# Products with c of five double tiles made ahead in a fused convolution and spectral-mix kernel, and stored tiles put in other places

## Chip, cores, metric

One core of a Trainium2 chip. The metric is the device time of one execution in microseconds, as a median of several runs. The profiler's span, from the first to the last instruction of one execution, is about 1.8 us shorter.

In the views, PE is the TensorE engine with its matmuls, DVE is VectorE, ACT is ScalarE, and POOL is GpSimd, which here issues most of the DMAs. SBUF is the memory that DMAs and engines share, PSUM the one into which PE writes. "X <-Y" in brackets is an idle time and what ended it.

## The reference, cut to what matters

```python
# x: (8, 3264, 192); w: softmax over 7 taps for 8 groups of 24 channels
x = causal_conv(x, w)                          # _attn_ref
X = rfft(x, axis=1)[:, :64]                    # 64 modes
Y = X @ (w_r + 1j * w_i)  per mode             # the weights: 64 x 192 x 192, twice
y = irfft(Y, n=3264)
u = x + y
out = u + relu(u @ w_ch)
```

The kernel never forms u @ w_ch from u. It adds c = x @ w_ch and y @ w_ch in PSUM.

## The kernel before

Three stages follow each other: the convolution with the forward transform (to about 72 us), the mixing with the weights, which come in 16 groups (to about 107 us), and the output stage. The output stage runs over items. Most are double tiles: two tiles of 128 rows for two batches, 384 KB of output. One item is made of the half tiles ("h") and three are "zw" tiles for the inverse transform. Each item takes one of four PSUM tiles of two banks in turn. The names C, M0 and M1 below are the parts of PE's work for an item. The code is cut and simplified; the cuts are marked by "...".

```python
xall  = sb("xall", [NSLOT, 2, D], BF16, align_bytes=256)
arena = sb("arena", [NW * WGB], BF16, align_bytes=256)   # weights, later stored tiles
cc    = sb("cc", [NQ, CB, P], BF16)                      # x transposed, for C
band  = sb("band", [H, 2 * P], BF16)                     # taps of the convolution
NO = 6
outs = [arena[:, OB * i:OB * (i + 1)]... for i in range(NO)]   # six places of 3072 bytes
outs.append(band[...])                                         # and one for the halves
...
def c_part(n):      # C: 12 matmuls, c of a double tile
    ... matmul(zt[:, i, D*k:D*k+D], cc[r, q, 3*t+j, :], wc[r, j, :], start=(k == 0 and j == 0))
def m_part(n, which):   # M0 = y @ w_ch, M1 = y: 4 matmuls of 384 columns each
def relu(n):        # ScalarE, in place in PSUM, 128x768 f32
def finish(n):      # VectorE adds x into a stored tile in SBUF, then a DMA stores it
...
for n in range(N + 1):
    m_part(n, 0); relu(n)
    if duos[n + 2] == ("h",): nc.scalar.copy(out=<PSUM tile of n + 2>, in_=halves)
    c_part(n + 1)
    m_part(n - 1, 1); finish(n - 1)
```

Of the kernel before, what the change touches and what calls it, by code (L numbers as in the profile page):

```python
# [12 lines left out]
F32 = mybir.dt.float32  # L13
# [6 lines left out]
def kernel(  # L20
# [9 lines left out]
    nc = tc.nc  # L30
    B, S, D = x.shape
# [5 lines left out]
    P = 128  # L37
# [15 lines left out]
    def sb(name, shape, dtype, **kw):  # L53
        return pool.tile([P] + shape, dtype, tag=name, name=name, **kw)
# [4 lines left out]
    NW = 4  # L59
    WGB = 4 * 3 * D  # L60
    arena = sb("arena", [NW * WGB], BF16, align_bytes=256)

    CB = 3 * NT
    cc = sb("cc", [NQ, CB, P], BF16)
# [13 lines left out]
    band = sb("band", [H, 2 * P], BF16)  # L78
# [3 lines left out]
    wc = sb("wc", [3, D], BF16)  # L82
# [11 lines left out]
    def wbuf(g):  # L94
        return wts[g] if g < NW + NL else wts[(g - NW - NL) % NW]

    NO = 6
    OB = 2 * 2 * 2 * D
    outs = [arena[:, OB * i:OB * (i + 1)].bitcast(F32).rearrange("p (k d) -> p k d", k=2) for i in range(NO)]
    assert NO * OB <= NW * WGB  # L100

    outs.append(band[:, :, :].rearrange("p h c -> p (h c)")[:, 0:OB].bitcast(F32).rearrange("p (k d) -> p k d", k=2))
    pos = [0]

    def temp(n, dtype):
# [36 lines left out]
    def slot(q, t):  # L142
        return NT * q + t
# [210 lines left out]
    tbank = [0]  # L354
    ncopy = [0]

    def copy(out, in_):
        ncopy[0] += 1
        if ncopy[0] % 3 == 0:
            nc.scalar.copy(out=out, in_=in_)  # L360
        else:
            nc.vector.tensor_copy(out=out, in_=in_)  # L362

    ring = low[2:4]

    def next_bank():
        z = ring[tbank[0] % len(ring)]
        tbank[0] += 1
        return z[:, :].bitcast(BF16)
# [29 lines left out]
    def some(n, upto=NT * NQ):  # L399
        for _ in range(n):  # L400
            if tjobs and tjobs[0][0] < upto:
                _, f, *a = tjobs.pop(0)
                f(*a)
# [3 lines left out]
    for k, u in enumerate(units):  # L407
# [5 lines left out]
        if k:  # L413
            q, t0, n = units[k - 1]
# [19 lines left out]
    def mix(g):  # L434
        yp = low[(g // 2) % 2][:, D * (g % 2):D * (g % 2) + D]
        for j in range(3):
            for p4 in range(4):
                m = 4 * g + p4
                nc.tensor.matmul(yp[32 * p4:32 * p4 + 2 * B, :], xt[:, j, :, m],  # L439
                                 wbuf(g)[:, p4, j, :], start=(j == 0), stop=(j == 2),  # L440
                                 tile_position=(0, 32 * p4), skip_group_check=True)
        if g < NW:
            load_w(g + NW + NL)
        elif g >= NW + NL:
            load_w(g + NW)
            if g + NW == NG - 1:

                small(0)
                small(1)

    def mix_copy(d, gs=slice(0, 2)):
        nc.scalar.copy(out=ymix[d % 2][:, gs, :],
                       in_=low[d % 2][:, 0:2 * D].rearrange("p (g d) -> p g d", g=2)[:, gs, :])
# [25 lines left out]
    ROWS = (LO, UP)  # L479
# [4 lines left out]
    def c_halves():  # L484
        for k in range(2):
# [8 lines left out]
                                         tile_position=(r.start, h.start))  # L494
            copy(halves[:, 2 * k:2 * k + 2, :], z[:, 0:2 * D].rearrange("p (a d) -> p a d", a=2))

    def c_part(n, ks=(0, 1)):
        duo, zt = items[n]
        for k, (q, t) in enumerate(duo):
            for j in range(3) if k in ks else ():  # L500
                for i, r in enumerate(ROWS):
                    nc.tensor.matmul(zt[:, i, D * k:D * k + D], cc[r, q, 3 * t + j, :], wc[r, j, :],  # L502
                                     start=(k == 0 and j == 0), stop=False, skip_group_check=True)
# [28 lines left out]
    def zw_copy(dst, src, act):  # L532
        if act:
            nc.scalar.activation(out=dst, in_=src, func=ACT.Copy, scale=ascale[:, 0:1])
        else:
            nc.vector.tensor_scalar(out=dst, in0=src, scalar1=ascale[:, 0:1], scalar2=None, op0=ALU.mult)

    duos = [((q, t), (q, t + 1)) for q in range(2) for t in (0, 2)]
# [3 lines left out]
    for k, item in ((2, 1), (8, 2), (11, 3), (14, ("h",))):  # L542
        duos.insert(k, item)

    buffers = []
    for duo in duos:
        buffers.append(NO if duo == ("h",) else sum(b < NO for b in buffers if b is not None) % NO
                       if isinstance(duo, tuple) else None)

    def relu(n):  # L550
        duo, zt = items[n]
        w = D * len(duo) if duo[0] != "h" else 2 * D
        nc.scalar.activation(out=zt[:, :, 0:w], in_=zt[:, :, 0:w], func=ACT.Relu)  # L553

    def finish(n):
        duo, zt = items[n]
        o = outs[buffers[n]]
        if duo[0] == "h":
            nc.vector.tensor_tensor(out=o[:, :, :].rearrange("p k (a d) -> p k a d", a=2),
                                    in0=zt[:, :, 0:2 * D].rearrange("p k (a d) -> p k a d", a=2),  # L560
                                    in1=xall[:, NF:NF + NT * (NQ - 1) + 1:NT, 0, :].rearrange(
                                        "p (k a) d -> p k a d", k=2), op=ALU.add)
            for k in range(2):
                for h, r in enumerate(ROWS):
                    dst = bass.AP(tensor=out.tensor, offset=out.offset + ((4 * k + (h ^ k)) * S + P * NF) * D,
                                  ap=[[D, HALF], [2 * S * D, 2], [1, D]])
                    nc.sync.dma_start(out=dst, in_=o[r, k, :].rearrange("p (a d) -> p a d", a=2))
            return
        (q0, t0), (q1, t1) = duo[0], duo[-1]
        s = [slot(*u) for u in duo]  # L570
        ov = o[:, :, :].rearrange("p k (i d) -> p (k i) d", i=2)
        if len(duo) == 1:
            nc.vector.tensor_tensor(out=ov[:, 0:2, :], in0=zt[:, :, 0:D], in1=xall[:, s[0], :, :], op=ALU.add)
            dst = bass.AP(tensor=out.tensor, offset=out.offset + (2 * q0 * S + P * t0) * D,
                          ap=[[D, P], [S * D, 2], [1, D]])
            (nc.gpsimd if n < N - 1 else nc.sync).dma_start(out=dst, in_=ov[:, 0:2, :])
            return
        nc.vector.tensor_tensor(out=o[:, :, :].rearrange("p k (i d) -> p i k d", i=2),  # L578
                                in0=zt[:, :, 0:2 * D].rearrange("p i (k d) -> p i k d", k=2),
                                in1=xall[:, s[0]:s[1] + 1:s[1] - s[0], :, :].rearrange("p k i d -> p i k d"),  # L580
                                op=ALU.add)
        if t0 == t1:

            dst = bass.AP(tensor=out.tensor, offset=out.offset + (2 * q0 * S + P * t0) * D,
                          ap=[[D, P], [S * D, 4], [1, D]])
            nc.gpsimd.dma_start(out=dst, in_=ov)  # L586
        else:
            for i in range(2):
                dst = bass.AP(tensor=out.tensor, offset=out.offset + ((2 * q0 + i) * S + P * t0) * D,
                              ap=[[D, P], [P * D, 2], [1, D]])  # L590
                nc.sync.dma_start(out=dst, in_=ov[:, i:4:2, :])

    N = len(duos)
    items = [[duo, None] for duo in duos]
# [3 lines left out]
            if k % 4 in Z:  # L598
                item[1] = Z[k % 4]

    PLAN = (2, 2, 1, 2, 2, 2, 1, 2, 3, 3, 3, 3, 3, 3, 99)
    for g in range(NG - 1):
        mix(g)
        if g == NG - 2:
            mix_copy(g // 2, slice(0, 1))
        elif g % 2:
            mix_copy(g // 2)
        some(PLAN[g], NT * (NQ - 1) if g < NW + NL - 1 else NT * NQ)
        if g == NG - 2:
            c_halves()  # L610
        if g == NG - 2:
            mix_trans(g // 2, slice(0, 1))
        elif g % 2:
            mix_trans(g // 2)
# [20 lines left out]
    def is_duo(n):  # L635
        return 0 <= n < N and isinstance(duos[n], tuple)

    for n in range(N + 1):
        if is_duo(n):
            m_part(n, 0)  # L640
            relu(n)
        if n + 2 < N and duos[n + 2] == ("h",):
            nc.scalar.copy(out=items[n + 2][1][:, :, 0:2 * D].rearrange("p k (a d) -> p k a d", a=2),
                           in_=halves.rearrange("p (k a) d -> p k a d", k=2))
        if n + 1 < N and n > 0:
            if is_duo(n + 1):
                if duos[n + 1] != ("h",):
                    c_part(n + 1)
            else:
                q, zt = items[n + 1]  # L650
                for c in range(2):
                    zw_part(q, c, zt[:, c, :])
                for act, w in enumerate(QUARTERS):
                    zw_copy(zw[:, q, :, w, :], zt[:, :, 0:2 * D].rearrange("p c (b e) -> p c b e", b=4)[:, :, w, :],
                            act)
        if is_duo(n - 1):
            m_part(n - 1, 1)
            finish(n - 1)
# [30 lines left out]
```

## Time and profile before

| | before |
|---|---|
| median of 6 runs | 180.06 us (179.76 to 180.76) |
| span of the profiled run | 178.0 us |
| last group of weights starts on PE | 106.93 us |
| last store issued | 172.22 us |
| PE, DVE, ACT busy from 150 to 160 us | 10.00, 8.45, 6.88 of 10 us |

The prediction below shows the lines that lead to its reading. One view that it read: busy time by stretch. Its columns are the stretch and its length, then the busy time of PE, PE's weight loads, DVE, ACT and POOL (with instructions), the granted clock, the DMA share, and GB/s.

```profile
140.00:144.00 4.00, 4.00 (x76) 3.15 (x72) 3.44 (x4) 2.94 (x4) 2.82 (x4) 1.00 0.98 373
...
148.00:152.00 4.00, 4.00 (x76) 3.15 (x74) 3.44 (x4) 2.92 (x4) 2.83 (x4) 1.00 0.91 344
...
156.00:160.00 4.00, 4.00 (x77) 3.15 (x74) 3.44 (x4) 2.90 (x4) 2.82 (x4) 1.00 0.90 344
```

PE is full and sets the pace. The DMA engines are at 0.90 to 0.98, so the stores keep up with little to spare: at 373 GB/s for a share of 0.98, full use would be about 380 GB/s by this estimate.

### The profile page before, as it was taken

To read this page: it belongs to the slowest core of one execution; us is meant where nothing else is said; L and a number is where in the kernel's file an instruction comes from. 1 tells how busy PE (TensorE), PEld (TensorE's weight loads), DVE (VectorE), ACT (ScalarE), POOL (GpSimd) and SP (SyncE) were. 2 spreads that over 40 slices of the span, in tenths; PEclk is the share of its full clock that TensorE was granted. 3 is DMA by queue.
4 is the path that set the end of the run, shared out by engine and by line. 5 is a ranking of instruction groups with operands and counts; after the bars stand their busy time and mean duration, and the time that the engine had idled before them with its cause. 6 is when DMAs were issued, how large, how long until landed. Compare 5 with 4: busy or idle time off the path is not lost.

```text
span 178.0 us, 6299 instructions
## 1 busy us (share of the span) xinstructions
PE 146.5 (82%) x2736; PEld 105.9 (59%) x2736; DVE 114.1 (64%) x163; ACT 99.5 (56%) x136; POOL 100.4 (56%) x155
## 2 busy tenths in 40 slices
PE   0047569999999999689967679999999999999930
PEld 0033346667666666467756556965777777777720
DVE  1878555675765576255454453796688888888870
ACT  8176653735553734365546355767766667766620
POOL 7999997867855624354226100035364766665760
PEclk9999987999999999999999999999999999999997
DMA  4999999999999999999999980296699899998894
GB/s 44 168 177 188 189 190 190 192 193 190 191 191 190 205 206 208 205 206 208 205 207 206 206 130 0 90 324 258 251 300 351 317 368 356 354 349 348 336 356 186
DMA packets 44331, 40.17 MB, mean 226 GB/s; under 512 B 28800, under 2 KB 40656, under 8 KB 44304
## 3 DMA queue, kind: packets, MB, share of 16 engines
q0 software_dynamic: 41136, 37.59, 106.0%
q1 hardware_dynamic: 3168, 2.19, 3.9%
q8 instruction: 21, 0.34, 0.7%
q14 instruction: 6, 0.05, 0.1%
HBM read 39.40 MB, written 20.05 MB: 334 GB/s over the span
## 4 chain that ended last, share of the span: by engine, by line
DMA 33%; POOL 32%; PE 16%; issue 13%; ACT 1%; POOLq 1%; DVE 1%; DVEq 0%
DMA arena<-in_moe_w_i_dram 19%; POOL out_dram L586 17%; POOL xall L151 10%; DMA xall<-in_x_dram 8%; DMA cc<-in_moe_w_i_dram 6%; PE z L307 4%; PE low L333 3%; PE za L522 2%; PE za L502 2%; POOL xall L221 1%; POOL arena L428 1%; PE zb L522 1%; PE zb L502 1%; ACT xall L325 1%; PE low L387 1%
## 5 line engine op out<-in xcount | busy, mean ns | idle before, releaser
L586 POOL DMA_DIRECT2D out_dram<-arena x45 | 33.9, 754 | 39.2 <-DVE arena L578 38.4
L151 POOL DMA_DIRECT2D xall<-in_x_dram x48 | 38.5, 813 | 6.7 <-DMA xall<-in_x_dram 4.6
L307 PE MATMUL z<-xall,band 64*64 64x192 bf16 (+3 forms) x816 | 27.8, 264 | 16.1 <-ACT band L195 10.5
L327 DVE CAST xall<-z 128x768 bf16<-128x768 f32 (+1 forms) x24 | 24.5, 1021 | 15.1 <-PE z L307 13.3
L307 PEld LDWEIGHTS <-band 64*64 64x64 bf16 x816 | 18.4, 111 | 24.8 <-ACT band L195 10.9
L325 ACT CAST xall<-z 128x768 bf16<-128x768 f32 (+1 forms) x24 | 20.4, 851 | 22.3 <-PE z L307 21.1
L502 PEld LDWEIGHTS <-cc 64*128 64x128 bf16 x600 | 26.2, 94 | 7.0 <-issue 1.2
L578 DVE TENSOR_TENSOR arena<-za,xall 128x768 f32<-128x768 f32 x26 | 24.8, 956 | 5.6 <-ACT zb L553 1.9
L553 ACT ACTIVATE za<-za 128x768 f32<-128x768 f32 (+1 forms) x27 | 21.0, 782 | 8.3 <-PE za L522 8.3
L578 DVE TENSOR_TENSOR arena<-zb,xall 128x768 f32<-128x768 f32 x23 | 21.9, 956 | 4.6 <-ACT za L553 1.8
L553 ACT ACTIVATE zb<-zb 128x768 f32<-128x768 f32 (+1 forms) x25 | 19.6, 782 | 8.4 <-PE zb L522 8.2
L333 PE MATMUL low<-xall,ftab 128*128 128x384 bf16 x100 | 21.7, 344 | 0.0
L387 PEld LDWEIGHTS <-xall 128*128 128x128 bf16 x300 | 18.7, 105 | 3.2 <-issue 0.3
L362 DVE COPY cc<-r 128x1024 bf16<-128x1024 bf16 (+2 forms) x18 | 11.2, 658 | 12.8 <-PE r L387 3.9
L502 PE MATMUL za<-wc,cc 64*128 64x192 bf16 x318 | 17.8, 243 | 0.0
L522 PE MATMUL za<-mixa,fsin 64*128 64x384 bf16 (+1 forms) x120 | 17.6, 304 | 0.0
L522 PE MATMUL za<-mixa,ftab 64*128 64x384 bf16 (+1 forms) x120 | 17.6, 304 | 0.0
L428 POOL DMA_DIRECT2D arena<-in_moe_w_r_dram x12 | 7.4, 615 | 15.4 <-PE low L439 10.3
L522 PE MATMUL zb<-mixa,ftab 64*128 64x384 bf16 (+1 forms) x100 | 15.6, 313 | 0.4 <-ACT zb L553 0.4
L502 PE MATMUL zb<-wc,cc 64*128 64x192 bf16 x282 | 15.6, 243 | 0.1
L522 PE MATMUL zb<-mixa,fsin 64*128 64x384 bf16 (+1 forms) x100 | 15.6, 313 | 0.0
L522 PEld LDWEIGHTS <-ftab 64*128 64x128 bf16 x220 | 11.0, 94 | 4.6 <-issue 1.7
(111 smaller groups left out, 184.2 us busy)
## 6 DMA issues: line engine op xcount, KB each, us to landing
out_dram<-arena POOLq DMA_DIRECT2D x45, 384.0 KB, 4.3
xall<-in_x_dram POOLq DMA_DIRECT2D x24, 192.0 KB, 7.4
xall<-in_x_dram POOLq DMA_DIRECT2D x16, 240.0 KB, 7.1
arena<-in_moe_w_r_dram POOLq DMA_DIRECT2D x12, 288.0 KB, 9.6
arena<-in_moe_w_i_dram POOLq DMA_DIRECT2D x12, 288.0 KB, 10.5
out_dram<-arena SPq DMA_DIRECT2D x9, 192.0 KB, 2.1
xall<-in_x_dram POOLq DMA_DIRECT2D x8, 144.0 KB, 7.1
cc<-in_moe_w_r_dram POOLq DMA_DIRECT2D x4, 288.0 KB, 11.5
```

The costliest lines, as they stand in the source:

```text
L151: nc.gpsimd.dma_start(out=xall[:, s0:s0 + nf, i, :], in_=src)
L307: mm = nc.tensor.matmul(ov[c], band[r, h, c.start + shift + 64 * (r is UP and c is LO): c.start + shift + 64 * (r is UP and c is LO) + 64] ...
L325: nc.scalar.copy(out=dst, in_=srcv)
L327: nc.vector.tensor_copy(out=dst, in_=srcv)
L333: nc.tensor.matmul(xp, ftab[:, t, :], xall[:, slot(q, t), :, :], start=(t == 0), stop=False, skip_group_check=True)
L362: nc.vector.tensor_copy(out=out, in_=in_)
L387: nc.tensor.transpose(tp[:, P * k:P * k + P], src, ident[:])
L502: nc.tensor.matmul(zt[:, i, D * k:D * k + D], cc[r, q, 3 * t + j, :], wc[r, j, :], start=(k == 0 and j == 0), stop=False, skip_group_check ...
L522: nc.tensor.matmul(zt[:, i, D * k:D * (k + w)], tabs[c][r, t, :], zw[r, q:q + w, c, QUARTERS[which], :], start=False, stop=end and k + w = ...
L553: nc.scalar.activation(out=zt[:, :, 0:w], in_=zt[:, :, 0:w], func=ACT.Relu)
L578: nc.vector.tensor_tensor(out=o[:, :, :].rearrange("p k (i d) -> p i k d", i=2), in0=zt[:, :, 0:2 * D].rearrange("p i (k d) -> p i k d", k=2),
L586: nc.gpsimd.dma_start(out=dst, in_=ov)
```

## The change

The output stage is bound by PE, and PE has room while the weights load. So the change makes C of five double tiles (items 6, 9, 12, 17, 20) in the weights' stretch and keeps it in f32 in SBUF. ScalarE copies it into the PSUM tile when its item is due. The kept products need room in the arena, so the stored tiles get other places too: two in the part of cc that is used up first, and one in the convolution's band. The transposes in the weights' stretch move to earlier groups.

```diff
-    NO = 6
-    outs = [arena[:, OB * i:OB * (i + 1)]... for i in range(NO)]
-    outs.append(band[...])
+    slices = [place(arena[:, OB * i:OB * (i + 1)]) for i in range(6)]
+    in_band = place(band[:, :, :].rearrange("p h c -> p (h c)")[:, 0:OB])
+    in_cc = [place(cc[:, q, 0:12, :].rearrange("p k s -> p (k s)")) for q in range(2)]
...
+    def c_ahead(n):          # C of item n into two banks, then two copies to AHEAD[n]
...
+    AHEAD = {6: in_band, 9: slices[0], 12: slices[1], 17: slices[2], 20: slices[3]}
+    FREED = {9: (6,), 13: (9, 12, 17), 14: (20,)}        # after which group of weights
+    free = [in_cc[0], slices[4], slices[5], in_cc[1]]
+    for n, duo in enumerate(duos):
+        if n + 1 in AHEAD:
+            free.insert(0, AHEAD[n + 1])
+        buffers.append(None)
+        if isinstance(duo, tuple):
+            buffers[n] = free.pop(0)
+            free.append(buffers[n])
...
-    PLAN = (2, 2, 1, 2, 2, 2, 1, 2, 3, 3, 3, 3, 3, 3, 99)
+    PLAN = (2, 2, 3, 2, 3, 2, 2, 2, 3, 3, 3, 3, 99, 99, 99)
...
+        if n + 2 in AHEAD:
+            nc.scalar.copy(out=items[n + 2][1][:, :, 0:2 * D], in_=AHEAD[n + 2])
-                if duos[n + 1] != ("h",):
+                if duos[n + 1] != ("h",) and n + 1 not in AHEAD:
                     c_part(n + 1)
```

More of the change, by code (lines that the diff above doesn't have):

```diff
@@ L95, in wbuf, with place @@
         return wts[g] if g < NW + NL else wts[(g - NW - NL) % NW]
-    NO = 6
     OB = 2 * 2 * 2 * D
-    outs = [arena[:, OB * i:OB * (i + 1)].bitcast(F32).rearrange("p (k d) -> p k d", k=2) for i in range(NO)]
-    assert NO * OB <= NW * WGB
-    outs.append(band[:, :, :].rearrange("p h c -> p (h c)")[:, 0:OB].bitcast(F32).rearrange("p (k d) -> p k d", k=2))
+    assert 6 * OB <= NW * WGB and OB == 12 * P
+    def place(a):
+        return a.bitcast(F32).rearrange("p (k d) -> p k d", k=2)
+    slices = [place(arena[:, OB * i:OB * (i + 1)]) for i in range(6)]
+    in_band = place(band[:, :, :].rearrange("p h c -> p (h c)")[:, 0:OB])
+    in_cc = [place(cc[:, q, 0:12, :].rearrange("p k s -> p (k s)")) for q in range(2)]
     pos = [0]
@@ L495, in c_halves @@
             copy(halves[:, 2 * k:2 * k + 2, :], z[:, 0:2 * D].rearrange("p (a d) -> p a d", a=2))
+    def c_ahead(n):
+        duo = duos[n]
+        zs = []
+        for i in range(2):
+            next_bank()
+            zs.append(ring[(tbank[0] - 1) % len(ring)])
+        for k, (q, t) in enumerate(duo):
+            for j in range(3):
+                for i, r in enumerate(ROWS):
+                    nc.tensor.matmul(zs[i][:, D * k:D * k + D], cc[r, q, 3 * t + j, :], wc[r, j, :],
+                                     start=(k == 0 and j == 0), stop=(k == 1 and j == 2), skip_group_check=True)
+        for i in range(2):
+            copy(AHEAD[n][:, i, :], zs[i][:, 0:2 * D])
     def c_part(n, ks=(0, 1)):
@@ L543 @@
         duos.insert(k, item)
+    AHEAD = {6: in_band, 9: slices[0], 12: slices[1], 17: slices[2], 20: slices[3]}
+    FREED = {9: (6,), 13: (9, 12, 17), 14: (20,)}
+    free = [in_cc[0], slices[4], slices[5], in_cc[1]]
     buffers = []
-    for duo in duos:
-        buffers.append(NO if duo == ("h",) else sum(b < NO for b in buffers if b is not None) % NO
-                       if isinstance(duo, tuple) else None)
+    for n, duo in enumerate(duos):
[5 more added lines that the diff above has]
+            free.append(buffers[n])
     def relu(n):
@@ L556, in finish @@
         duo, zt = items[n]
-        o = outs[buffers[n]]
+        o = buffers[n]
         if duo[0] == "h":
@@ L608 @@
         some(PLAN[g], NT * (NQ - 1) if g < NW + NL - 1 else NT * NQ)
+        for n in FREED.get(g, ()):
+            c_ahead(n)
         if g == NG - 2:
```

## The prediction

> **What bounds the kernel now.** I read the busy row by slices first, then the chain that ended last, then the timeline of three places: the weights' stretch, the start of the output stage, and one period of it. The page gives this:
>
> ```profile
> PE   0047569999999999689967679999999999999930
> DMA  4999999999999999999999980296699899998894
> GB/s 44 168 177 188 189 190 190 192 193 190 191 191 190 205 206 208 205 206 208 205 207 206 206 130 0 90 324 258 251 300 351 317 368 356 354 349 348 336 356 186
> ```
>
> A slice is 4.45 us. Until 106 us the DMA engines never rest (206 GB/s, loads of x and of the weights). Then comes a short pause of DMA, and from 112 us to the end the results are stored, with PE in nines all the way. So there are two stages with two bounds. The timeline of the weights' stretch shows what its groups wait for:
>
> ```profile
> 101.21 0.46 PE L439 MATMUL low<-arena,mixa 128*16 128x192 bf16 x12 [0.97 <-DMA arena<-in_moe_w_i_dram]
> ...
> 104.08 0.46 PE L439 MATMUL low<-arena,mixa 128*16 128x192 bf16 x12 [0.72 <-DMA arena<-in_moe_w_i_dram]
> ...
> 106.93 0.46 PE L439 MATMUL low<-arena,mixa 128*16 128x192 bf16 x12 [0.23 <-DMA arena<-in_moe_w_i_dram]
> ```
>
> Groups of weights arrive every 2.87 us and PE stands idle 0.7 to 1.0 us before each: this stage is bound by the load, and PE has room. One period of the output stage, from its timeline:
>
> ```profile
> 133.92 0.33 PE L522 MATMUL zb<-mixa,fsin 64*128 64x384 bf16 x2
> ...
> 134.02 0.96 DVE L578 TENSOR_TENSOR arena<-za,xall 128x768 f32<-128x768 f32 x1 [0.19 <-ACT za L553]
> 134.09 0.66 PE L502 MATMUL zb<-wc,cc 64*128 64x192 bf16 x12
> ...
> 134.58 0.33 PE L522 MATMUL za<-mixa,ftab 64*128 64x384 bf16 x2
> ...
> 134.91 0.33 PE L522 MATMUL zb<-mixa,ftab 64*128 64x384 bf16 x2
> ...
> 135.23 0.66 PE L502 MATMUL za<-wc,cc 64*128 64x192 bf16 x12
> ...
> 135.44 0.80 ACT L553 ACTIVATE zb<-zb 128x768 f32<-128x768 f32 x1 [0.35 <-PE zb L522]
> ```
>
> From start to start, C (the 12 products with c, L502) takes 134.58 - 134.09 = 0.49 us, M1 (the second 4 products of the item before) 134.91 - 134.58 = 0.33, and M0 (the first 4 products of an item) 135.23 - 134.91 = 0.32. The period is 135.23 - 134.09 = 1.14 us and the three fill it: PE bounds this stage. In the same period ACT works 0.80 (relu) and DVE 0.96 (the last add). The chain of waits follows the storing queue on POOL through here; but POOL works 0.75 of each 1.14 us and waits for DVE in between, so it only follows PE's pace.
>
> **What the Trainium skill says.** "TensorE: Matmul & The Clock Gate", Part 1, gives N / 2.4 GHz + 2.5 ns from matmul to matmul: 82 ns for 192 columns, 162 ns for 384. The trace agrees if the two 64-row halves run side by side: 6 pairs x 82 = 0.49 us for C, 2 pairs x 162 = 0.33 for M0 or M1. "ScalarE: Activation LUTs", What ACT_TABLE_LOAD costs: 186 ns + 0.833 ns per element, back-to-back ones overlapping by about 93 ns; for 768 elements 826 ns, 733 in a row. The trace has 0.80 us, and 0.74 from start to start where two follow each other (123.38 to 124.12 us). "PSUM — Partial Sum Buffer", The four PSUM rules: ScalarE's writes leave the accumulate bits alone, so the matmuls after it add onto the written data only where earlier matmuls left the bits set; the item of halves already works so in the kernel before, so I expect right results. "DMA: Bandwidth & Descriptors", Anatomy of one DMA: about 2.0 us + bytes / 436 GB/s, 2.9 us for a 384 KB store; the trace's fastest store took 2.9 us, the median 4.3.
>
> **The change, part by part.** (a) Removed from the output stage: C of items 6, 9, 12, 17 and 20. 5 x 0.49 = 2.45 us of PE. This is the most that can be gained: 1.4% of 180.2.
>
> (b) Added there: five ScalarE copies of 128x768 f32 from SBUF to PSUM, 0.80 us each. The same copy stands in the trace for the item of halves, and PE waited for it:
>
> ```profile
> 123.38 0.80 ACT L643 COPY zb<-cc 128x768 f32<-128x768 f32 x1
> ...
> 124.23 0.36 PE L514 MATMUL zb<-mixa,ftab 64*64 64x384 bf16 x4 [0.25 <-ACT zb L643]
> ```
>
> (c) Added in the weights' stretch: 5 x 12 matmuls, 0.49 us a dozen, and 10 copies of 128x384 f32 (0.63 us on DVE, about 0.48 on ACT). One dozen comes after group 9, three after group 13, one after 14. In exchange the transposes move to earlier groups: groups 13 and 14, which now carry three banks (1.52 us of PE) and one (0.7), carry none. At group 13 that is 3 x 0.49 = 1.47 for 1.52. The third dozen needs the two banks of the first back, estimated at 103.0 us, so it ends at about 103.55 and the transpose of the mixed rows at 103.95, just before group 14 lands (104.08). At group 14: 0.46 + 0.49 + 24 small products (1.0) + 0.3 ends at about 106.3, before 106.93. Earlier, four banks more by group 6 (4 x 0.56 = 2.2 us of PE) delay group 8 from 87.1 to about 89.3 and the next load's issue with it; by then some 5 us of loads are queued (issue to landing takes 10 us), and PE has caught up by group 12. So this part costs nothing on the path, with 0.1 to 0.6 us to spare.
>
> (d) Stored tiles in other places: 4 buffers at first, 9 at the end, for 6. The shortest turn is 5 items, over 5 us, against 3 to 4 us to landing at that time. No effect.
>
> **What a copied item really gains.** The copy of item m can't come early. It follows relu(m-2) on ACT, and its PSUM tile is free when DVE's add of item m-4 has ended. In steady running these two fall together; I put M0(m-1) at 134.91. Then relu(m-2) ends at 134.29 + 0.74 = 135.03 and the add of m-4 at 134.02 + 0.96 = 134.98. The copy runs from 135.03 to 135.83, visible at about 135.88. PE without C does M0(m-1) to 135.23, M1(m-2) to 135.56 and would start M0(m) there: it waits 0.33 us. The gain is 0.49 - 0.33 = 0.16 us. The next relu starts 0.35 late but still makes its M1, at about 136.6 for 136.7. PE, at its bound, makes up nothing of the stall later.
>
> For items 6, 9 and 12 I went through the timeline the same way, adding 0.74 to ACT for each copy: M0(6) at 115.32 for 115.51 (gain 0.19), M0(9) at 118.61 for 118.86 (0.25 in all), M0(12) at 121.78 for 122.05 (0.27 in all). Here zw tiles (0.58 us of ACT each) and DVE's adds hold PE too: in the trace C(10) starts when the add of item 6 ends. The item of halves then waits for its own copy, which waits for the add of item 10, only 0.16 us earlier than before. Item 17 has the add of item 13 ahead of it, which is late in the trace (126.15), and gains about nothing; item 20 gains 0.16. **Sum: 0.16 + 0 + 0.16 = about 0.3 us.** The last stores follow the last add as before (5 us). I round to 0.4: 179.8 us.
>
> **Rivals.** (1) *The whole 2.45 us comes through* (177.8): ACT is idle 0.35 us per period, and the copies lie 3, 3, 5 and 3 items apart, so on average ACT has room. Against it: a copy must fit between two given moments, and the halves' copy already stalls PE. I give a gain of over 1.2 us one chance in ten. (2) *ACT becomes the bound in items 7 to 14*: five relus 4.0, two zw 1.2, the halves' relu and copy 1.5, two copies 1.5: 8.2 us against 7.6 of PE before. If this adds up without slack it costs 0.6 us: 180.8. Its four PSUM tiles should absorb it. (3) *The weights' stretch grows*, as copies on DVE or ACT hold up a bank and PE comes late to group 14 or 15: up to +0.5 us, 180.5. (4) *Stores become the bound*: 384 KB per 1.14 us is 343 GB/s, while the trace reaches 370 in five microseconds; a gain of 2.45 us over 50 would ask for about 360. This would only cut a gain of rival 1.
>
> **Range and chances.** Even the full gain is 1.4%, and no loss above adds to 3.6 us, so over 2% either way would need something I don't see. Runs of the kernel before spread from 180.0 to 180.8. I take 178.9 to 180.7.
>
> **What would show it.** Right: in the changed trace PE waits about 0.3 us for ACT's copy before the first products of items 6, 9, 12, 17 and 20; the last group of weights still starts near 106.9; the last add comes 0.2 to 0.8 us earlier. Wrong: no such waits and PE's stage shorter by about 2 us (rival 1); DVE or ACT ahead of the last groups of weights, which then start after 107.3 (rival 3); the item of halves later than before (rival 2); adds waiting for stores (the buffers).

## The result, and the profile after

The changed kernel is right, and takes 181.55 us (median of 6 runs, 181.22 to 182.19) against 180.06. The ratio is 1.0085, with a 95% interval from 1.0057 to 1.0112. Ratios here are the mean time of one kernel's fast runs over the mean of the other's in the same rounds, so they are not quite the ratios of the medians. Executions over 1.5% slower than the fastest of the same kernel are left out of the means. The change costs about 1.5 us, and 181.55 us lies outside the predicted range of 178.9 to 180.7.

The busy rows of the page of the changed kernel:

```profile
PE   0047569999999999699998889997999999999900
...
DMA  4999999999999999999999960577798999999993
GB/s 47 163 168 188 190 190 189 192 193 189 191 191 190 206 206 208 204 207 207 205 204 206 207 101 4 175 265 276 266 302 334 306 361 339 354 360 328 366 319 146
```

DMA is now in nines nearly all the way from the slice at 130 us to the end, and yet the GB/s are no higher. The groups of weights, from the timeline of PE:

```profile
101.44 0.45 PE L443 MATMUL low<-arena,mixa 128*16 128x192 bf16 x12 [0.31 <-DMA arena<-in_moe_w_i_dram]
...
104.28 0.46 PE L443 MATMUL low<-arena,mixa 128*16 128x192 bf16 x12
...
107.16 0.46 PE L443 MATMUL low<-arena,mixa 128*16 128x192 bf16 x12 [0.77 <-DMA arena<-in_moe_w_i_dram]
```

The last group starts at 107.16 us and PE has waited 0.77 us for its data. So the added work doesn't hold it up. The copies from the same timeline:

```profile
118.84 0.34 PE L541 MATMUL za<-mixa,ftab 64*128 64x384 bf16 x2 [0.25 <-ACT za L674]
...
121.99 0.34 PE L541 MATMUL za<-mixa,ftab 64*128 64x384 bf16 x2 [0.21 <-ACT za L674]
...
131.42 0.34 PE L541 MATMUL za<-mixa,ftab 64*128 64x384 bf16 x2 [0.16 <-ACT za L674]
```

PE waits for ScalarE's copy before the first products of items 9, 12 and 20, as predicted. The view counts a wait only from the modelled end of the matmuls before, and prints none for items 6 and 17. By the start times in the timelines of PE and ACT, the first products of all five begin 0.04 to 0.06 us after their copy ends. In the order of the items that is 0.25, 0.42, 0.38, 0.09 and 0.34 us later than the usual 0.16 after the pair of matmuls before. Four intervals close the account:

| us, profiled runs | before | changed | difference |
|---|---|---|---|
| start of the last group of weights | 106.93 | 107.16 | +0.23 |
| from there to the issue of the last store | 65.29 | 65.02 | -0.27 |
| from there to the end of the span | 5.8 | 7.5 | +1.7 |
| span | 178.0 | 179.7 | +1.7 |

The output stage's work is 0.27 us shorter, close to the 0.3 of the prediction's sum. All of the loss comes after the last store is issued. The view of the storing line shows the time from issue to landing of the last two stores, first before, then changed:

```profile
DMA to landing us min/median/max: 4.3/4.3/4.4
```

```profile
DMA to landing us min/median/max: 5.6/5.8/6.0
```

The DMA engines come to the end with a backlog. The same stretches as before, in the changed kernel:

```profile
140.00:144.00 4.00, 4.00 (x75) 3.33 (x72) 3.44 (x4) 2.95 (x4) 2.82 (x4) 1.00 0.99 307
...
148.00:152.00 4.00, 4.00 (x76) 3.35 (x72) 3.44 (x4) 2.95 (x4) 2.83 (x4) 1.00 1.00 351
...
156.00:160.00 4.00, 4.00 (x76) 3.37 (x72) 3.44 (x4) 2.95 (x4) 2.82 (x4) 1.00 1.00 379
```

The share stays at 0.99 to 1.00 while the rate goes from 307 to 379 GB/s. The engines are busy all the time and sometimes move less. The finer stretches show a rhythm:

```profile
148.17:149.31 1.14, 1.14 (x26) 0.95 (x22) 0.95 (x2) 0.79 (x2) 0.75 (x2) 1.00 1.02 391
...
150.46:151.61 1.15, 1.15 (x26) 0.96 (x22) 0.96 (x2) 0.80 (x2) 0.76 (x2) 1.00 0.98 313
151.61:152.75 1.14, 1.14 (x26) 0.95 (x22) 0.95 (x2) 0.79 (x2) 0.75 (x2) 1.00 0.97 296
152.75:153.90 1.15, 1.15 (x26) 0.96 (x22) 0.96 (x2) 0.80 (x2) 0.76 (x2) 1.00 0.98 309
...
155.04:156.19 1.15, 1.15 (x26) 0.96 (x22) 0.96 (x2) 0.80 (x2) 0.76 (x2) 1.00 1.01 386
```

Three periods of about 300 GB/s come back every 10.3 us, which is nine periods of 1.145 us, and nine is the number of places. Three of the nine are not in the arena. They are issued shortly before, as the timeline of POOL shows:

```profile
147.83 0.75 POOL L615 DMA_DIRECT2D out_dram<-cc  x1 [0.39 <-DVE cc L607]
148.97 0.76 POOL L615 DMA_DIRECT2D out_dram<-band  x1 [0.39 <-DVE band L607]
150.12 0.75 POOL L615 DMA_DIRECT2D out_dram<-cc  x1 [0.39 <-DVE cc L607]
```

So stores out of cc and band seemed to be slow. The packet records in the trace, which no view prints, say the same directly. These stores move in packets of 4,608 bytes. Counted off in order of start, 80 to a store of 384 KB, the median packet took 178 to 192 ns in each store out of the arena and 216 to 231 ns in each out of cc or band. The addresses in the compiled program gave a theory. The arena starts at 97,536, a multiple of 256. cc starts at 116,032 and band at 219,712, both 64 bytes past a multiple of 256. **Theory A:** the start address costs. **Theory B:** the places or their number cost, for instance because PE reads its weights out of cc. **Theory C:** the added copies slow the DMA.

### The profile page after: what moved, and what is told of

The parts are those of the page before. It is cut to its first block, busy times and chain, and to the rows that moved or that the text cites. A ratio compares the mean times of both kernels' runs of the same rounds, so it can differ in the third digit from the quotient of the medians.

```text
span 179.7 us, 6326 instructions
## 1 busy us (share of the span) xinstructions
PE 148.7 (83%) x2736; PEld 109.3 (61%) x2736; DVE 116.9 (65%) x169; ACT 104.2 (58%) x145; POOL 100.3 (56%) x155
## 4 chain that ended last, share of the span: by engine, by line
PE 46%; POOL 19%; issue 14%; DVE 7%; DMA 5%; ACT 4%; POOLq 1%; DVEq 0%; ACTq 0%
POOL out_dram L615 17%; PE z L311 13%; PE low L337 9%; DMA arena<-in_moe_w_i_dram 5%; PE r L391 5%; PE low L391 4%; PE low L443 3%; PE r L380 3%; DVE arena L193 2%; PE za L541 2%; PE zb L541 1%; PE low L350 1%; DVE xall L331 1%; PE za L521 1%; POOL xall L155 1%
## 5 line engine op out<-in xcount | busy, mean ns | idle before, releaser
L615 POOL DMA_DIRECT2D out_dram<-arena x29 | 21.8, 752 | 13.6 <-DVE arena L607 11.5
L521 PEld LDWEIGHTS <-cc 64*128 64x128 bf16 x540 | 24.5, 94 | 6.1 <-issue 1.9
L541 PE MATMUL za<-mixa,ftab 64*128 64x384 bf16 (+1 forms) x120 | 18.3, 305 | 0.6 <-ACT za L674 0.6
L607 DVE TENSOR_TENSOR arena<-za,xall 128x768 f32<-128x768 f32 x16 | 15.3, 957 | 3.2 <-ACT zb L582 1.1
L541 PE MATMUL zb<-mixa,ftab 64*128 64x384 bf16 (+1 forms) x100 | 16.2, 313 | 0.5 <-ACT zb L582 0.4
L607 DVE TENSOR_TENSOR arena<-zb,xall 128x768 f32<-128x768 f32 x15 | 14.3, 956 | 3.4 <-ACT za L582 1.3
L541 PEld LDWEIGHTS <-ftab 64*128 64x128 bf16 x220 | 12.9, 94 | 6.0 <-issue 3.1
L541 PE MATMUL zb<-mixa,fsin 64*128 64x384 bf16 (+1 forms) x100 | 16.2, 313 | 0.0
L521 PE MATMUL za<-wc,cc 64*128 64x192 bf16 x270 | 15.4, 243 | 0.4 <-DVE arena L607 0.4
L366 DVE COPY cc<-r 128x1024 bf16<-128x1024 bf16 (+2 forms) x17 | 10.6, 657 | 6.6 <-PE r L391 3.6
```

The source lines that it names most:

```text
L366: nc.vector.tensor_copy(out=out, in_=in_)
L521: nc.tensor.matmul(zt[:, i, D * k:D * k + D], cc[r, q, 3 * t + j, :], wc[r, j, :], start=(k == 0 and j == 0), stop=False, skip_group_check ...
L541: nc.tensor.matmul(zt[:, i, D * k:D * (k + w)], tabs[c][r, t, :], zw[r, q:q + w, c, QUARTERS[which], :], start=False, stop=end and k + w = ...
L607: nc.vector.tensor_tensor(out=o[:, :, :].rearrange("p k (i d) -> p i k d", i=2), in0=zt[:, :, 0:2 * D].rearrange("p i (k d) -> p i k d", k=2),
L615: nc.gpsimd.dma_start(out=dst, in_=ov)
```

## The experiments

Twelve runs follow (aligned2 is aligned once more), on four chips, each with the kernel before beside them. The texts of what was expected: where they say 18 of 51 stores, 18 of the 49 double tiles is right. Each time stands beside the kernel before in the same rounds.

| run | edit, in a few words | median us | before us | ratio (95%) |
|---|---|---|---|---|
| aligned | changed kernel, cc and band at multiples of 256 | 179.52 | 180.08 | 0.9976 (0.995 to 1.0001) |
| aligned2 | the same again | 180.15 | 179.95 | 0.9998 (0.9966 to 1.0031) |
| places | the places alone, no products ahead | 181.92 | 180.08 | 1.0098 (1.0063 to 1.0134) |
| places_aligned | the same at multiples of 256 | 180.22 | 179.95 | 1.0024 (0.9979 to 1.0068) |
| shift32 | before, places 32 bytes higher | 187.93 | 180.08 | 1.044 (1.0411 to 1.0469) |
| shift64 | before, 64 bytes higher | 187.71 | 180.08 | 1.0418 (1.0389 to 1.0448) |
| shift128 | before, 128 bytes higher | 187.41 | 180.08 | 1.0398 (1.0364 to 1.0432) |
| shift192 | before, 192 bytes higher | 187.24 | 180.08 | 1.0399 (1.0372 to 1.0425) |
| aligned_nocopy | aligned, no copies (wrong result) | 179.94 | 180.08 | 0.9995 (0.9964 to 1.0025) |
| before_half | before, halved adds (wrong result) | 179.13 | 179.77 | 0.9946 (0.9909 to 0.9983) |
| aligned_half | aligned, halved adds (wrong result) | 178.24 | 179.77 | 0.9916 (0.9876 to 0.9955) |
| nocopy_half | no copies, halved adds (wrong result) | 177.37 | 179.77 | 0.9857 (0.9828 to 0.9886) |

### Does the start address cost? aligned and places

```diff
-    cc = sb("cc", [NQ, CB, P], BF16)
+    cc = sb("cc", [NQ, CB, P], BF16, align_bytes=256)
-    band = sb("band", [H, 2 * P], BF16)
+    band = sb("band", [H, 2 * P], BF16, align_bytes=256)
```

> The changed kernel with cc and band allocated at multiples of 256 bytes (in the changed kernel both start 64 bytes past one, the arena at a multiple); nothing else is edited. Theory A, the stores' source address: the stores from cc and band, 18 of 51, cost more DMA time because they start 64 bytes past a multiple of 256. Then the stretches at about 305 GB/s with full DMA share vanish, the share falls from 0.99 to about 0.92, stores land in 4.3 instead of 5.2 us, and the kernel takes 179.6 to 180.1 us, 0.1 to 0.5 below the kernel before. Theory B, the places themselves (PE reads its weights out of cc while stores read it) or the number of buffers in flight (9 for 6): no change, 181.5 us. Theory C, the five ScalarE copies or the ten copies more slow the DMA: no change, 181.5 us.

It took 179.52 us, just below the range of theory A. The places, their number, the products and the copies are all still there, so B and C fall. Stretches of aligned:

```profile
140.00:144.00 4.00, 4.00 (x76) 3.31 (x72) 3.44 (x4) 2.95 (x4) 2.74 (x4) 1.00 0.98 367
...
148.00:152.00 4.00, 4.00 (x76) 3.31 (x72) 3.44 (x4) 2.95 (x4) 2.77 (x4) 1.00 0.92 347
152.00:156.00 4.00, 4.00 (x74) 3.31 (x72) 3.25 (x5) 2.60 (x5) 2.49 (x4) 1.00 0.93 364
```

The share is back at 0.92 to 0.98. The lists of DMA issues of the changed kernel and then of aligned have as columns the size of a store and the median from issue to landing:

```profile
out_dram<-arena POOLq DMA_DIRECT2D x29, 384.0 KB, 5.2
...
out_dram<-cc POOLq DMA_DIRECT2D x11, 384.0 KB, 5.2
...
out_dram<-band POOLq DMA_DIRECT2D x5, 384.0 KB, 5.2
```

```profile
out_dram<-arena POOLq DMA_DIRECT2D x29, 384.0 KB, 4.3
out_dram<-cc POOLq DMA_DIRECT2D x11, 384.0 KB, 4.1
out_dram<-band POOLq DMA_DIRECT2D x5, 384.0 KB, 4.1
```

The stores of the arena land as late as the slow ones, 5.2 us, though their own median packets took 178 to 192 ns; so they seem to queue behind the slow ones on the same engines. That is why the list alone did not show which were slow; the fine stretches and the packet records did.

The run places takes the other half of the change away:

```diff
-        for n in FREED.get(g, ()):
-            c_ahead(n)
...
-        if n + 2 in AHEAD:
-            nc.scalar.copy(out=items[n + 2][1][:, :, 0:2 * D], in_=AHEAD[n + 2])
-                if duos[n + 1] != ("h",) and n + 1 not in AHEAD:
+                if duos[n + 1] != ("h",):
# and PLAN as before
```

> The changed kernel's places for stored tiles alone: no products ahead, no copies, the old plan of transposes, c made in the output stage as before. Theory A: the 1.5 us of loss is all there, plus the 0.3 that the products won: 181.5 to 181.9 us. Theory B the same. Theory C: 180.1 us as before.

It took 181.92 us: the places alone cost all of the loss. From its last store's issue (173.86 us) to the end of its span (181.2) it needs 7.3 us, like the changed kernel (7.5). Its profiled run, 182.97 us, was the slowest of the six, so only this interval is compared.

### The dose: shift64

Here the kernel before keeps its six places, and they start 64 bytes higher.

```diff
-    arena = sb("arena", [NW * WGB], BF16, align_bytes=256)
+    arena = sb("arena", [NW * WGB + 128], BF16, align_bytes=256)
-    outs = [arena[:, OB * i:OB * (i + 1)]...
+    SH = 32
+    outs = [arena[:, SH + OB * i:SH + OB * (i + 1)]...
```

> The kernel before with its six places for stored tiles moved 64 bytes up inside the arena, which is made 256 bytes longer; weights and everything else stay where they are. Theory A: every one of these stores is slow; at about 305 GB/s one of 384 KB takes 1.29 us against the period of 1.145, the stores become the bound, and over about 45 of them the kernel gets 4 to 7 us slower: 184 to 187 us. Theories B and C: no change, 180.1 us.

It took 187.71 us, above the 184 to 187 expected: 64 bytes cost 7.6 us. (The arena is 256 bytes longer, so the tensors behind it start 256 higher, as far past a multiple of 256 as before.) Its stretches:

```profile
148.00:152.00 4.00, 3.42 (x62) 2.69 (x59) 2.86 (x3) 2.27 (x3) 2.27 (x3) 1.00 0.99 305
152.00:156.00 4.00, 4.00 (x70) 3.09 (x68) 2.88 (x4) 2.50 (x5) 2.26 (x3) 1.00 1.00 298
```

The waits of DVE in it, which are new:

```profile
DVE arena L579 <- DMA out_dram<-arena: 6.8, 15, 1.1
```

The engines are full at about 300 GB/s. A store of 384 KB (393,216 bytes) then takes 1.31 us against the period of 1.145, and the difference times 45 stores is 7.4 us. DVE now waits for stores to free their places: the stores bound this kernel. Full use of the aligned engines, estimated at 380 GB/s (from 373 GB/s for a share of 0.98 in the kernel before), gives 1.03 us. So a start off the multiple costs a factor of about 1.27 by this estimate. The packet records agree: the median packet of 4,608 bytes took 178 ns in the kernel before and in aligned, and 225 to 227 ns in the four shifted kernels.

### Which rule: shift32, shift128, shift192

The edit is that of shift64 with SH = 16, 64 and 96 elements of two bytes.

> As shift64, but the six places start 32 bytes past a multiple of 256. Rule 1, the row of 768 bytes touches four blocks of 256 bytes instead of three: as slow as shift64, 187 to 188 us. Rule 2, the cost goes with the bytes fetched from the boundary below (800 for 768 here, 832 in shift64): only slightly slower than before, 180 to 184 us.

> 128 bytes past a multiple of 256. Rule 1: 187 to 188 us as shift64. Rule 2 (896 bytes fetched): slower than shift64, 190 us or more. Rule 3, only a start that is no multiple of 128 costs: 180.1 us as before.

> 192 bytes past a multiple of 256. Rule 1: 187 to 188 us. Rule 2 (960 bytes fetched): the slowest of all, over 192 us. Rule 3: as shift64, 187 to 188 us.

All three are as slow as shift64, within 0.7 us of each other, with the largest shift the fastest by a little. Of the three rules only rule 1 holds: among these four shifts it hardly matters how far the start lies past the multiple.

The Trainium skill has the piece that fits, in "DMA: Bandwidth & Descriptors", How a descriptor splits into AXI transactions: a descriptor (one piece of a DMA) is cut into transactions of 256 bytes that start at multiples of 256, and one that starts elsewhere begins its first transaction at the multiple below. The rows stored here are 192 floats, 768 bytes. From a multiple of 256 that is three transactions; from any of the four shifts it is four. Four for three would be a factor of 1.33, near the 1.27 measured. That the cost goes with this count is an inference from the page and the four times. It takes each row as a descriptor of its own (over a longer run of bytes one more transaction would weigh less); no run here shows the descriptors or counts transactions.

### Are the places otherwise free? places_aligned and aligned2

```diff
# places, with the two align_bytes=256 of aligned
```

> The changed kernel's places for stored tiles at multiples of 256 bytes, without the products ahead. If alignment is the whole cost of the places: as the kernel before within 0.3 us, 180.0 us. If places or the number of buffers had a cost or a gain of their own: it shows here.

> The aligned changed kernel once more, beside places_aligned on the same chip, to see whether the products win anything once the stores are at full pace: 0.3 to 0.6 us below both places_aligned and the kernel before (0.2 to 0.3%), or nothing.

With aligned starts the places cost nothing that can be seen (180.22 us against 179.95, the interval includes 1). The second run of aligned gave 180.15, and its ratio 0.9998 includes 1 as well. The 0.5 us that aligned seemed to win is not confirmed. What the products win is in the size of the runs' spread, so no version here clearly beats the kernel before.

### Why the five removed products win so little: aligned_nocopy and the halved adds

2.45 us of PE's work left the output stage, and 0.27 us came of it. The prediction put this down to the wait for the copy. The first test takes the copies away, so that the five items lack c:

```diff
# aligned, and
-        if n + 2 in AHEAD:
-            nc.scalar.copy(out=items[n + 2][1][:, :, 0:2 * D], in_=AHEAD[n + 2])
```

> Wrong result on purpose (the five items lack their products with c): the aligned changed kernel without the five ScalarE copies, which shows what the removed products are worth when nothing waits for a copy. My account of the prediction (each copy stalls PE by about 0.33 of the 0.49 us that it saves): PE's waits for copies go and the last add comes about 1.5 us earlier than in the aligned kernel, the time 178.2 to 178.8 us, unless the stores become the bound on the way. Rival, the copies stall nothing and the gain is lost elsewhere: as the aligned kernel, within 0.3 us.

This was a miss: 179.94 us, no faster than aligned, and 64.99 us from the last group of weights to the last store's issue, against 65.01. The waits of PE after items 9 and 12 have moved by one step, to C of the next item:

```profile
119.46 0.67 PE L521 MATMUL zb<-wc,cc 64*128 64x192 bf16 x12 [0.48 <-DVE cc L607]
...
122.99 0.67 PE L521 MATMUL za<-wc,cc 64*128 64x192 bf16 x12 [0.82 <-DVE arena L607]
```

PE, freed of C of item 9, comes early to C of item 10. That needs the PSUM tile of item 6, and DVE's last add hasn't left it yet. Four tiles go round, and their turn is nearly as long as PE's four periods: in the kernel before, an add that ends at 134.98 us is followed by the next C on its tile at 135.23, by the prediction's timeline. So a single removed C can win only about that 0.25 us before it meets the add, with or without a copy. To test this, three kernels halve the adds (0.55 us for 0.96), which frees the tiles some 0.4 us earlier:

```diff
-        nc.vector.tensor_tensor(out=o[...].rearrange("p k (i d) -> p i k d", i=2), in0=..., in1=...)
+        nc.vector.tensor_tensor(out=o[...].rearrange("p k (i d) -> p i k d", i=2)[:, 0:1],
+                                in0=...[:, 0:1], in1=...[:, 0:1])
```

> Wrong result on purpose: the kernel before with the halved adds, the baseline for the two others. PE bounds its output stage, so it is at most 0.8 us faster than the kernel before (shorter waits around the zw tiles and the halves, and a shorter last add): 179.3 to 180.1 us.

> Wrong result on purpose: the aligned changed kernel with DVE's last adds of double tiles cut to half their columns (0.55 us for 0.96), so that PSUM tiles come free some 0.4 us earlier; stores as before. With aligned_nocopy no faster than aligned, two limits are in question: the copy on ACT and the turn of the four PSUM tiles, which DVE's add ends. If ACT's copy alone holds PE (0.33 us each): within 0.4 us of before_half, about 0.3 less than it. If the turn of the tiles holds it as well: the copy can start when relu ends, which is no earlier, so also within 0.3 to 0.6 us of before_half.

> Wrong result on purpose: aligned_nocopy with the halved adds. If the turn of the PSUM tiles is the second limit: neither it nor a copy holds PE now, and most of the 5 x 0.49 us comes through, 1.4 to 2.4 us less than before_half. If something else limits (ACT's relus, PE's order): at most 0.5 us less than before_half, as aligned_nocopy against before.

before_half came out a little below its range (179.13 us for 179.3 to 180.1). From the last group of weights to the last store's issue, in the profiled runs (the two columns were taken in different calls, and the profile of before is older than both; the profiled run of aligned_half was the slowest of its four, its last group of weights started at 108.22 us, and the interval leaves that out):

| | full adds | halved adds |
|---|---|---|
| C in the stage (before) | 65.29 | 64.44 |
| C ahead, with copies (aligned) | 65.01 | 63.46 |
| C ahead, no copies (wrong result) | 64.99 | 62.41 |

With the adds out of the way, the products win 0.98 us with copies and 2.03 us without, of 2.45. aligned_half is 0.9 us below before_half in the medians too (178.24 and 179.13), which is more than the 0.3 to 0.6 expected. nocopy_half is 1.8 below it (177.37), as expected of a second limit. The waits of PE after 107 us agree: with full adds, C waits for DVE in aligned_nocopy (0.48 and 0.82 us); with halved adds no C waits for DVE any more, aligned_half still waits 0.21 us each for the copies of items 9 and 12, and nocopy_half for neither. So there are two limits, one close behind the other: the copy, and the turn of the PSUM tiles that the add ends.

## Why the prediction was wrong, point by point

- **The bounds of the stages: right.** The weights' stretch waits for its loads in the changed kernel too, and PE fills the output stage. One reading was off: "0.7 to 1.0 us before each" group holds for two of the three lines shown, and the last group waited only 0.23 us.
- **(a) and (b), removed products and copies: right in sum.** The stage is 0.27 us shorter for 0.3 predicted. By start times PE lost 0.34 us to the copy of item 20, for 0.33 in my steady sum. The last add started 0.12 us earlier than before (171.52 for 171.64), less than the 0.2 to 0.8 foretold, because the last group of weights came 0.23 us later. The other parts are less good than the sum, which agrees partly by luck. Counted from the last group of weights, the products of the halves start 0.18 us later than before (124.64 - 107.16 against 124.23 - 106.93) for 0.16 earlier predicted, and item 17 won about 0.3 for nothing. In the changed kernel the add of item 9 starts at 121.93 us, after products of item 10 instead of its own; I can't say why, and this stays open. The late halves were the sign named for rival 2 (ACT as the bound), but ACT stood idle 0.40 us before their copy until DVE's add of item 10 had ended, so ACT was not the bound there.
- **The reason for (b) was incomplete.** It named the copy as what holds PE and the add only as what holds the copy. aligned_nocopy shows the add holding PE as soon as the copy is gone, and the halved adds show that both must go.
- **(c) The weights' stretch: right.** The last group waited 0.77 us for its data. It started 0.23 us later than before, but with an unchanged weights' stretch it also started at 107.32 in before_half, so I don't charge this to the change.
- **(d) Stored tiles in other places, "No effect": the step that failed.** I counted how soon a place is used again and did not ask at which address it starts. Those stores pay about 1.27 times the DMA time. The arena and xall carry an alignment of 256 in the source, and cc and band do not; that was in the code to be read, and so was the page on transactions.
- **Rival 4, "This would only cut a gain of rival 1": wrong with it.** It took the stores' pace as given (370 GB/s). The sixteen large stores from cc and band and the four of half size make 18 of 384 KB, and 18 x 0.28 us is an estimate of 5.0 us more DMA work; the packets of 4,608 bytes alone took 4.3 us more, spread over the 16 engines. Most of it disappears in the idle share of the DMA engines; what is left is a backlog at the end, 1.7 us as measured.
- **"Within 2%" held; the range did not.** The slower side of the range had only the weights' stretch and the copies in it.

## What to carry to other kernels

When a change moves the buffers that DMAs read or write, compare the start addresses and not only the sizes and the reuse: here 32 to 192 bytes past a multiple of 256 cost about a quarter more DMA time for rows of 768 bytes. Here DMA engines with a busy share of 0.90 to 0.98 had too little room for stores that cost 1.27 times as much, and a share that rose to 1.00 while the GB/s did not rise was the sign of it. Before taking work off the bounding engine, ask how long the buffers' turn is: here the gain ended where the next buffer wasn't free yet, and taking away the first wait only showed the second.

## What the Trainium skill lacked or had wrong

- "DMA: Bandwidth & Descriptors", How a descriptor splits into AXI transactions, gives the cost of a start off a multiple of 256 in beats of 32 bytes, beside the count of transactions: by its rule, 24 beats for an aligned row of 768 bytes, 25 at a shift of 32 and 30 at 192. The runs show the same loss at both ends (187.93 and 187.24 us for 180.08). The page doesn't say which of the two sets the time. Here the count of transactions, four for three, fits, and the beats don't. The page has no measured rate for such a start; here about 300 GB/s against an estimated 380 at full share.
- The same page's table of rules for kernel authors has no row on the start address of an SBUF buffer that DMAs store from, and "SBUF — State Buffer", Operand start alignment, says of its own rule that it "is about legality, not speed". The speed decided: 18 of 49 double tiles stored from an unaligned start cost 1.5 us of 180, all of them 7.6.
- No page that I found says how a few slow transfers show up: all stores landed later together (5.2 us for 4.3), and only GB/s by fine stretches, beside the order of the issues, and the times of single packets (216 to 231 ns for 178 to 192) told which ones were slow.
